# The second plain chunk prepares the fast weights in another order: loads first, high parts later

## The chip, the cores and the metric

The kernel runs on one core of a Trainium2 chip. The metric is the device time of one execution in microseconds (us), the median of the runs shown. TensorE (PE) multiplies matrices, VectorE (DVE) and ScalarE (ACT) work on elements, GpSimd (POOL) does little here, and SyncE (SP) issues every transfer. Each engine, SP's queue of transfers too, works in the order in which its instructions were written.

## The reference

The reference is sigmoid attention followed by a block of Fourier mixing, layer norm and a feed-forward network, for 8 sequences of 448 tokens and a width of 768:

```
x  = sigmoid(q k^T / 8 - log 448) v            (12 heads of 64, joined)
u  = x + real(fft(fft(x, tokens), width))
un = (u - mean) / sqrt(var + 1e-6)
out = u + max(un w1, 0) w2                      (768 -> 3072 -> 768)
```

The weights come as float64, and the result must be better than one float16 product gives. So each operand of the feed-forward network is split into a high part (rounded to float16) and a low part (the rest, float16 again), and three products are summed: high by high, high by low, low by high.

## The kernel before, in words

The 3584 tokens are worked in 7 chunks of 512. First come attention and mixing; in them the first two chunks are normed. Then two *plain* chunks (c = 0 and 1) go through the feed-forward network with the ordinary three products, in 24 iterations f of 128 hidden columns each. The last five chunks use a *fast* scheme in which a 2 by 2 block product is made from 7 products instead of 8; for that it needs sums and differences of the weights' quarters.

Those sums are made while the second plain chunk runs, by `combine` (L666), one call per step n, for 24 weight chunks j = 0 to 23 (j % 2 tells w1 from w2, j // 2 the pair of 128 columns):

- n = 0: the load. A tile `cb` (tag "wr", **three buffers**, 768 KB) is read from `t_dram` (L670).
- n = 1: the sums. Four DVE subtractions in place, L678.
- n = 2: the high part `ch`, an ACT copy to float16 with the scale, L682, into a tile of tag "wt".
- n = 3: the low part `cl`, DVE, L687, into the next tile of tag "wt". That tag has **three buffers**, used in turn by ch and cl.
- n = 4: six stores to `w_dram` on SP's queue: ch and two copies of plain high weights, then cl and two copies of plain low weights (L696 to L698 for w1, L700 to L702 for w2).

An iteration f of the second chunk (loop at L767) writes on the engines, in this order: the up-projection on PE (`up_proj`, 18 matmuls into a PSUM bank `psh`), its evacuation (`evac`: `hh` on ACT, L596, and `hl` on DVE, L597), the steps of `combine` that the table `made_at` names, the steps of the first fast chunk's norm (`fast_norm`, table `norm_at`), and the down-projection of the iteration before (`down_proj`, 18 matmuls that read hh and hl). The banks of `psh` are two, and the norm's transposes `pst` (L726, iterations 6 to 8 and 17 to 19) take a bank from the same two; ACT empties those into `U` (L727). The norm's casts to float16 are L739 (ACT) and L743 (DVE). `pin()` at the end of an iteration fixes the written order on each engine.

There are 24 weight chunks for 20 iterations, so four iterations take two of them. Chunk j has its turn in iteration f(j): 1, 2, 3, 4, 5, 5, 6, 7, 8, 8, 9, 10, 11, 11, 12, 13, 14, 14, 15 and so on to 20. The doubles are the chunks 4 and 5, 8 and 9, 12 and 13, 16 and 17. Before the change, chunk j is loaded in iteration f(j) − 1, summed and rounded (n = 1, 2) in f(j), and its low part and stores (n = 3, 4) come in f(j) + 1. Within an iteration all of this stands behind the evacuation: first the low parts and stores of the earlier chunk, then the load of the next, then sums and high part.

Of the kernel before, what the change touches and what calls it, by code (L numbers as in the profile page):

```python
# [44 lines left out]
NPLAIN = 2  # L45
# [13 lines left out]
def spectral_attention_ffn(tc, q, k, v, w1, w2, cd, cs, ident_in, out):  # L59
# [8 lines left out]
    with ExitStack() as top:  # L68
# [19 lines left out]
        if True:  # L88
# [356 lines left out]
            def prep_step(k, n):  # L445

                loads = []
                for d in range(1, 5):
                    if k + d < len(order) and (k + d, 0) not in prepped and not loadable(k + d, k):
                        break  # L450
                    loads.append((d, 0))
                for d, m in (loads, ((1, 1),), ((0, 2), (-1, 4)), ((0, 3),))[n]:
                    if k + d < len(order) and (k + d, m) not in prepped:
                        prepped.add((k + d, m))
                        prep_w(*order[k + d], m)
# [114 lines left out]
        with ExitStack() as fast, ExitStack() as st, ExitStack() as early:  # L570
# [12 lines left out]
            def up_proj(c, f, part=range(NCC)):  # L583
                uh, ul = uts[c]
                if (c, f) not in hs:
                    hs[c, f] = ps_h.tile([128, 512], F32, tag="m", name="psh")
                for m in part:
                    for n, (l, r) in enumerate(((w1h, uh), (w1h, ul), (w1l, uh))):
                        nc.tensor.matmul(  # L589
                            hs[c, f], l[f][:, m], r[:, m], start=(m == n == 0), stop=(m == NCC - 1 and n == 2))  # L590

            def evac(c, f):
                ps = hs[c, f]
                hh = up.tile([128, TW], F16, tag="hh", name="hh")
                hl = up.tile([128, TW], F16, tag="hl", name="hl")
                nc.scalar.activation(hh, ps, AF.Relu)  # L596
                nc.vector.scalar_tensor_tensor(  # L597
                    out=hl, in0=ps, scalar=0.0, in1=hh, op0=ALU.max, op1=ALU.subtract)
                hs[c, f] = (hh, hl)

            def down_proj(c, f):
                hh, hl = hs.pop((c, f))
                for n, cuts in enumerate(BANKS):
                    for i, lo, hi, at in cuts:
                        cols = slice(i * 128, (i + 1) * 128)

                        for m, (l, r) in enumerate(((hh, w2h), (hh, w2l), (hl, w2h))):
                            nc.tensor.matmul(  # L608
                                po[n][:, at:at + hi - lo], l[:, cols], r[f][:, lo:hi],
                                start=(f == 0 and m == 0 and at == 0),  # L610
                                stop=(f == NFC - 1 and m == 2 and at + hi - lo == 512))
                    if f == NFC - 1:
                        finish(c, n)
# [3 lines left out]
            def residual(c, g):  # L617
                u = wpre.tile([128, DM, 2], I32, tag="wr", name="ur", bufs=3).bitcast(F32)
                urs[c, g] = u = u.rearrange("p n w -> p (n w)").rearrange("p (i n) -> p i n", i=2)
                r0 = c * TW + g * 256  # L620
                nc.sync.dma_start(u, u_dram[r0:r0 + 256, :].rearrange("(i p) n -> p i n", p=128))
# [22 lines left out]
            while units or act_next or dve_next or sp_next:  # L644
# [4 lines left out]
                n = step % MIX_STEP  # L649
# [16 lines left out]
            def combine(i, p, n):  # L666

                if n == 0:
                    made[i, p] = t = wpre.tile([128, 4, 384], F32, tag="wr", name="cb", bufs=3)
                    nc.sync.dma_start(t.rearrange("p s n -> p (s n)"), t_dram[i, p].rearrange("p j n -> p (j n)"))  # L670
                elif n == 1:
                    t = made[i, p]
                    for o, x, y, op in (
                            ((1, 0, 1, ALU.add), (0, 2, 0, ALU.subtract),
                             (2, 1, 2, ALU.subtract), (3, 3, 2, ALU.subtract)),
                            ((2, 3, 2, ALU.subtract), (3, 1, 3, ALU.subtract),
                             (1, 1, 2, ALU.subtract), (0, 0, 1, ALU.subtract)))[i]:
                        nc.vector.tensor_tensor(out=t[:, o], in0=t[:, x], in1=t[:, y], op=op)  # L678
                elif n == 2:
                    t = made[i, p]  # L680
                    h = wpre.tile([128, 4, 384], F16, tag="wt", name="ch", bufs=3)
                    nc.scalar.activation(h, t, AF.Copy, scale=wsc[:, i:i + 1])  # L682
                    made[i, p] = t, h
                elif n == 3:
                    t, h = made[i, p]
                    l = wpre.tile([128, 4, 384], F16, tag="wt", name="cl", bufs=3)
                    nc.vector.scalar_tensor_tensor(  # L687
                        out=l, in0=t, scalar=wsc[:, i:i + 1], in1=h, op0=ALU.mult, op1=ALU.subtract)
                    made[i, p] = h, l
                else:  # L690
                    for j, (x, b) in enumerate(zip(made.pop((i, p)), ((w1h, w1l), (w2h, w2l))[i])):
                        to = w_dram[i, p][:, j]
                        b = [(b[f].rearrange("p c f -> p (c f)") if i == 0 else b[f]).rearrange(
                            "p (s n) -> p s n", s=2) for f in (2 * p + 1, 2 * p)]
                        if i == 0:
                            nc.sync.dma_start(to[:, 3:7], x)  # L696
                            nc.sync.dma_start(to[:, 0:1], b[0][:, 1:2])
                            nc.sync.dma_start(to[:, 1:3], b[1])  # L698
                        else:
                            nc.sync.dma_start(to[:, 0:4], x)  # L700
                            nc.sync.dma_start(to[:, 4:6], b[0])
                            nc.sync.dma_start(to[:, 6:7], b[1][:, 0:1])  # L702
# [44 lines left out]
            def load_w(i, P):  # L747
                if P < NP * (NCK - NPLAIN):
                    ws[i, P] = t = fw[i].tile([128, 2, 7, 384], F16, tag="ws", name="ws", bufs=(2, 4)[i])
                    nc.sync.dma_start(t, w_dram[i, P % NP])  # L750


            norm_at, made_at = {}, {}
            for j in range(NFC):
                f = 1 + j - (j > 4) - (j > 8) - (j > 12) - (j > 16)
                made_at.setdefault(f - 1, []).append((j, 0))
                made_at.setdefault(f, []).extend((j, n) for n in (1, 2))
                made_at.setdefault(f + 1, []).extend((j, n) for n in (3, 4))
            for x in made_at.values():
                x.sort(key=lambda x: (x[1] < 3, x[1] > 0, x))  # L760
            for tp in range(2):
                for f, steps in enumerate(((0,), (), (1, 2), (3, 4, 5, 6, 7), (8, 9), (), (10,), (11,), (12,),
                                           (13, 14), (15, 16), (17,))):
# [1 line left out]
            prev = None  # L765
            for c in range(NPLAIN):
                for f in range(NFC):  # L767
                    if (c, f) not in hs:
                        up_proj(c, f)
                    for n in range(2):  # L770
                        if c == 0 and slot <= len(order):
                            for step in range(4):
                                prep_step(slot, step)
                            slot += 1
                        if n == 0 and (c or f):
                            evac(c, f)
                    if f in (NFC - 3, NFC - 2):
                        residual(c, f - NFC + 3)
                    if c == NPLAIN - 1:
                        for j, n in made_at.get(f, ()):  # L780
                            combine(j % 2, j // 2, n)
                    if c == NPLAIN - 1:
                        for tp, n in norm_at.get(f, ()):
                            fast_norm(NPLAIN, tp, n, ps_h)
                    if prev is not None:
                        down_proj(*prev)
                    prev = (c, f)
                    pin()
                    if c == NPLAIN - 1 and f == NW1 + 1:
                        early.close()  # L790
                        fw.append(fast.enter_context(tc.tile_pool(name="fw1", bufs=1)))
                        h_pool = fast.enter_context(tc.tile_pool(name="h_pool", bufs=4))
                    if c == NPLAIN - 1 and f in (NFC - 4, NFC - 2):
                        load_w(0, (f - NFC + 4) // 2)
# [217 lines left out]
```

## Time and profile before

| what | value |
|---|---|
| median of 3 runs | 1744.54 us (1743.26 to 1745.85) |
| span of the profiled execution | 1744.9 us |
| PE busy | 1659.8 us, 95% of the span |
| DVE busy | 1296.0 us, 74% |
| ACT busy | 601.7 us, 34% |
| second plain chunk, 694 to 892 us | 198.0 us, PE busy 182.59 |
| 24 loads `cb`, 768 KB each | 6.4 us to landing (median) |
| 24 stores of `ch`, 384 KB each | 4.9 us to landing (median) |

The profile is one execution. In its views a row of a timeline gives the start in us, the duration, the engine, the line, the operation with out<-in, the count, and in brackets how long the engine had been idle before and what ended that. A row "SPq" is a transfer being issued; its landing is told by the view of the transfers. A releaser is inferred: where two things end together, the row names one of them.

### The profile page before, as it was taken

The numbers are of one execution on the slowest core, as the hardware profiler recorded it, in microseconds if no ns is written. First come the engines' busy times: TensorE is split into PE (matmuls) and PEld (weight loads), VectorE is DVE, ScalarE is ACT, GpSimd is POOL, SyncE is SP. The second block draws the span as 40 slices with busy tenths as digits, with TensorE's granted clock in tenths as the row PEclk, the third lists the DMA queues.
The fourth block names the chain that finished last, engine by engine and source line by source line (L and its number), as shares of the span: only waits on it lengthen the run. The fifth ranks groups of instructions, "written<-read, shape, count | busy, mean of one in ns | idle before, by whom it ended". The sixth has DMA issues, their size and how long they took to land. (4 is left out here: it accounts for less than half of the span.)

```text
span 1744.9 us, 27688 instructions
## 1 busy us (share of the span) xinstructions
PE 1659.8 (95%) x10996; PEld 1070.3 (61%) x10996; DVE 1296.0 (74%) x2481; ACT 601.7 (34%) x767; POOL 201.8 (12%) x220
## 2 busy tenths in 40 slices
PE   8999999997879999998899999999999999999997
PEld 4555555554544445554467777777777777777774
DVE  4556677866788884768557888788878888887768
ACT  5444444443334441232224332323232333223221
POOL 4534543443300000000000000000000000000000
PEclk9999999998999999999999999999999999999999
DMA  7666766874477663788876555655565665665561
GB/s 237 224 218 202 244 215 223 266 222 125 151 247 245 227 213 145 252 321 282 280 275 268 208 227 206 252 220 224 201 256 218 227 234 205 249 239 222 202 245 50
DMA packets 109140, 391.02 MB, mean 224 GB/s; under 512 B 23522, under 2 KB 49363, under 8 KB 93523
## 3 DMA queue, kind: packets, MB, share of 16 engines
q1 hardware_dynamic: 109010, 389.26, 63.4%
q8 instruction: 86, 1.41, 0.3%
q14 instruction: 44, 0.35, 0.1%
HBM read 312.15 MB, written 73.92 MB: 221 GB/s over the span
## 5 line engine op out<-in xcount | busy, mean ns | idle before, releaser
L870 PE MATMUL pso<-ws,H 128*128 128x384 f16 x2520 | 422.6, 326 | 0.9 <-DVE H L825 0.8
L819 PE MATMUL psf<-ut,ws 128*128 128x256 f16 x3780 | 422.1, 273 | 1.1 <-DVE ur L629 1.1
L819 PEld LDWEIGHTS <-ws 128*128 128x128 f16 x3780 | 369.8, 98 | 50.4 <-issue 1.4
L870 PEld LDWEIGHTS <-H 128*128 128x128 f16 x2520 | 246.4, 98 | 155.8 <-DVE H L825 1.1
L136 ACT ACTIVATE a<-sc 112x900 f32<-112x900 f32 x192 | 166.8, 918 | 154.2 <-PE sc L132 153.9
L879 DVE TENSOR_TENSOR acc<-pso,acc 128x384 f32<-128x384 f32 x350 | 181.6, 548 | 19.1 <-PE pso L870 19.1
L844 ACT ACTIVATE F<-F 128x1024 f32<-128x1024 f32 x60 | 63.5, 1058 | 332.1 <-DVE F L825 332.1
L152 PE MATMUL av<-a,vr 112*64 112x450 f32 x768 | 171.7, 569 | 3.5 <-DVE xT L161 3.5
L825 DVE TENSOR_TENSOR H<-F,H 128x1024 f16<-128x1024 f32 x120 | 129.4, 1087 | 47.0 <-ACT H L854 47.0
L589 PE MATMUL psh<-ut,w1h 128*128 128x512 f16 x504 | 152.1, 384 | 5.9 <-DVE hl L597 5.9
L608 PE MATMUL po<-w2h,hh 128*128 128x512 f16 (+1 forms) x384 | 128.9, 336 | 19.0 <-ACT hh L596 16.3
L825 DVE TENSOR_TENSOR F<-X,psf 128x256 f32<-128x256 f32 x240 | 97.8, 417 | 51.6 <-PE psf L819 48.9
L854 ACT ACTIVATE H<-F 128x1792 f16<-128x1792 f32 x60 | 101.8, 1697 | 88.6 <-DVE F L825 88.6
L608 PE MATMUL po<-w2h,hl 128*128 128x512 f16 (+1 forms) x384 | 128.5, 335 | 1.0
L608 PE MATMUL po<-w2l,hh 128*128 128x512 f16 (+1 forms) x384 | 128.5, 335 | 0.0
L608 PEld LDWEIGHTS <-hh 128*128 128x128 f16 x768 | 76.2, 100 | 71.5 <-ACT hh L596 21.0
L161 DVE TENSOR_SCALAR xT<-av 128x450 f32<-128x450 f32 x48 | 30.0, 625 | 115.5 <-PE av L152 115.5
L825 DVE TENSOR_TENSOR F<-F 128x256 f32<-128x256 f32 x240 | 91.1, 421 | 17.3 <-ACT F L844 12.9
L597 DVE SCALAR_TENSOR_TENSOR hl<-psh,hh 128x512 f16<-128x512 f32 x48 | 33.1, 690 | 94.7 <-ACT hh L596 94.5
L132 PE MATMUL sc<-qh,kh 64*112 64x450 f32 x384 | 82.6, 426 | 20.0 <-ACT a L136 15.3
L152 PEld LDWEIGHTS av<-a,vr 112*64 112x64 f32 x768 | 48.0, 140 | 84.1 <-issue 70.0
L589 PE MATMUL psh<-ut,w1l 128*128 128x512 f16 x252 | 96.5, 383 | 0.0
(105 smaller groups left out, 1977.2 us busy)
## 6 DMA issues: line engine op xcount, KB each, us to landing
ws<-w_dram SPq DMA_DIRECT2D x120, 1344.0 KB, 6.1
wr<-w_in SPq DMA_DIRECT2D x74, 768.0 KB, 6.0
cb<-t_dram SPq DMA_DIRECT2D x24, 768.0 KB, 6.4
t_dram<-wt SPq DMA_DIRECT2D x38, 384.0 KB, 2.6
qr<-q_in SPq DMA_DIRECT2D x48, 225.0 KB, 4.3
kr<-k_in SPq DMA_DIRECT2D x48, 224.0 KB, 3.6
vr<-v_in SPq DMA_DIRECT2D x24, 448.0 KB, 4.6
spare<-w_in SPq DMA_DIRECT2D x12, 768.0 KB, 4.7
```

The costliest lines, as they stand in the source:

```text
L132: nc.tensor.matmul(ps[:CP, j, :SQ], split[g, 1, kn][h, c * CP:(c + 1) * CP], split[g, 0, qn][h], start=(n == 0), stop=(n == 2))
L136: nc.scalar.activation(a, ps[:CP, :, :SQ], AF.Sigmoid, bias=-math.log(S), scale=1.0 / math.sqrt(D))
L152: nc.tensor.matmul(ps[j * D:(j + 1) * D, :SQ], vr[:, c, h * D:(h + 1) * D], a[:, j], start=(c == 0), stop=(c == 3))
L589: nc.tensor.matmul(hs[c, f], l[f][:, m], r[:, m], start=(m == n == 0), stop=(m == NCC - 1 and n == 2))
L597: nc.vector.scalar_tensor_tensor(out=hl, in0=ps, scalar=0.0, in1=hh, op0=ALU.max, op1=ALU.subtract)
L608: nc.tensor.matmul(po[n][:, at:at + hi - lo], l[:, cols], r[f][:, lo:hi], start=(f == 0 and m == 0 and at == 0), stop=(f == NFC - 1 and m ...
L819: nc.tensor.matmul(ps[:, :TH], w[:, x, a, m * 128:(m + 1) * 128], ut[y][:, b, m], start=(m == n == 0), stop=(m == n == 2))
L825: nc.vector.tensor_tensor(out=o, in0=x, in1=y, op=op)
L844: nc.scalar.activation(F[:, 0:4], F[:, 0:4], AF.Relu)
L854: nc.scalar.activation(hts[P][:, 0], F[:, 1:8], AF.Copy)
L870: nc.tensor.matmul(ps[:, :384], H[:, x, a, tp * 128:(tp + 1) * 128], w[:, y, b], start=(j == n == 0), stop=(j == 1 and n == 2))
L879: later(0, lambda: nc.vector.tensor_tensor(out=to, in0=ps[:, :384], in1=to, op=ALU.add))
```

## The change

Each step gets a place within the iteration: 0 is ahead of the up-projection, 1 and 2 are behind the evacuation, in that order. The load of chunk j goes to place 0 of iteration f(j) − 1 (it stood behind the stores there), the high part goes to place 0 of iteration f(j) + 1 (it stood behind the sums in f(j)), low part and stores stay in f(j) + 1, and the sums stay in f(j), behind them.

```
-                made_at.setdefault(f - 1, []).append((j, 0))
-                made_at.setdefault(f, []).extend((j, n) for n in (1, 2))
-                made_at.setdefault(f + 1, []).extend((j, n) for n in (3, 4))
-            for x in made_at.values():
-                x.sort(key=lambda x: (x[1] < 3, x[1] > 0, x))
+                made_at.setdefault((f - 1, 0), []).append((j, 0))
+                made_at.setdefault((f + 1, 0), []).append((j, 2))
+                made_at.setdefault((f + 1, 1), []).extend((j, n) for n in (3, 4))
+                made_at.setdefault((f, 2), []).append((j, 1))
...
                 for f in range(NFC):
+                    if c == NPLAIN - 1:
+                        for j, n in made_at.get((f, 0), ()):
+                            combine(j % 2, j // 2, n)
                     if (c, f) not in hs:
                         up_proj(c, f)
...
                     if c == NPLAIN - 1:
-                        for j, n in made_at.get(f, ()):
-                            combine(j % 2, j // 2, n)
+                        for k in (1, 2):
+                            for j, n in made_at.get((f, k), ()):
+                                combine(j % 2, j // 2, n)
```

The order of the instructions on PE and on DVE is the same before and after. On SP's queue and on ACT it differs. First SP's queue at the double of chunks 4 and 5, iteration 6, before; `ch_6411` and `cl_6466` are the high and low part of chunk 4, `ch_6417` and `cl_6474` those of chunk 5, and `cb_6482` is the load of chunk 7. The brackets list the engines and earlier transfers that a transfer waits for; a wait that an earlier one in the queue covers is not repeated.

```order
376 L696 DMA w_dram_62<-cl_6466 128x1536 [waits DMAHW7_49,DVE_49]
377 L697 DMA w_dram_62<-w1l5_4333 128x384 [waits DMAHW0_49]
378 L698 DMA w_dram_62<-w1l4_4332 128x768 [waits DMAHW1_49]
379 L700 DMA w_dram_62<-ch_6417 128x1536 [waits DMAHW2_49,Activation_49]
380 L701 DMA w_dram_62<-w2h5_4555 128x768 [waits DMAHW3_49]
381 L702 DMA w_dram_62<-w2h4_4554 128x384 [waits DMAHW4_49]
382 L700 DMA w_dram_62<-cl_6474 128x1536 [waits DMAHW5_49,DVE_49]
383 L701 DMA w_dram_62<-w2l5_4576 128x768 [waits DMAHW6_49]
384 L702 DMA w_dram_62<-w2l4_4575 128x384 [waits DMAHW7_49]
385 L670 DMA cb_6482<-t_dram_61 128x1536 [waits DMAHW0_49]
```

The store of the high part of chunk 4 stands three rows ahead of this piece and waits for ACT alone; the load of chunk 7 stands behind all stores of chunks 4 and 5. The same place after; here `cb_6443` is the load of chunk 7, `ch_6439` and `cl_6468` are the parts of chunk 4:

```order
372 L702 DMA w_dram_62<-w2l2_4350 128x384 [waits DMAHW3_49]
373 L670 DMA cb_6443<-t_dram_61 128x1536 [waits DMAHW4_49,DVE_49,Activation_49]
374 L696 DMA w_dram_62<-ch_6439 128x1536 [waits DMAHW5_49]
375 L697 DMA w_dram_62<-w1h5_4319 128x384 [waits DMAHW6_49]
376 L698 DMA w_dram_62<-w1h4_4318 128x768 [waits DMAHW7_49]
377 L696 DMA w_dram_62<-cl_6468 128x1536 [waits DMAHW0_49]
```

The load of chunk 7 has moved ahead of both stores of chunk 4, and the waits for ACT and DVE have moved from those stores to the load.

Second, ACT in iterations 5 to 8, before; `ch_6411` and `ch_6417` are the high parts of chunks 4 and 5, `ch_6488` and `ch_6559` those of 6 and 7, `hh_6462`, `hh_6539` and `hh_6610` belong to iterations 6, 7 and 8:

```order
380 L682 ACTIVATE ch_6411<-cb_6338,wsc_65 128x1536
381 L682 ACTIVATE ch_6417<-cb_6340,wsc_65 128x1536
382 L596 ACTIVATE hh_6462<-psh_6443 128x512
383 L682 ACTIVATE ch_6488<-cb_6405,wsc_65 128x1536
384 L727 ACTIVATE U_6061<-pst_6490 128x4x128
385 L596 ACTIVATE hh_6539<-psh_6520 128x512
386 L682 ACTIVATE ch_6559<-cb_6482,wsc_65 128x1536
387 L727 ACTIVATE U_6061<-pst_6561 128x4x128
388 L596 ACTIVATE hh_6610<-psh_6591 128x512
```

And after, where the high parts of chunks 4 to 7 are `ch_6439`, `ch_6441`, `ch_6518` and `ch_6589`:

```order
380 L682 ACTIVATE ch_6439<-cb_6307,wsc_65 128x1536
381 L682 ACTIVATE ch_6441<-cb_6309,wsc_65 128x1536
382 L596 ACTIVATE hh_6464<-psh_6445 128x512
383 L727 ACTIVATE U_6061<-pst_6488 128x4x128
384 L682 ACTIVATE ch_6518<-cb_6374,wsc_65 128x1536
385 L596 ACTIVATE hh_6543<-psh_6524 128x512
386 L727 ACTIVATE U_6061<-pst_6559 128x4x128
387 L682 ACTIVATE ch_6589<-cb_6443,wsc_65 128x1536
388 L596 ACTIVATE hh_6612<-psh_6593 128x512
```

Only ch and U have changed places; where an iteration has no work of the norm on ACT, the two orders are the same.

## The prediction

> **What bounds the kernel now.** I read the page's head first, then the table of windows, then the timelines of PE, ACT, DVE and the DMA queue where the second plain chunk combines the weights, and last the landing times of single transfers. Durations below come from the profiled execution; all that is shown of its time is its span, 0.4 us over the median of the runs, 1744.54 us, so the sum is made on the median.
>
> ```profile
> span 1744.9 us, 27688 instructions
> ```
>
> The edit touches the iterations between about 694 and 892 us. The table of windows, cut where TensorE stops (columns: length, then busy time and instructions of PE, PEld, DVE, ACT, POOL, then the granted clock, the DMA share and GB/s):
>
> ```profile
> 734.00:754.00 20.00, 15.83 (x78) 8.13 (x76) 11.04 (x14) 6.66 (x7) 0.00 (x0) 0.91 0.86 305
> 790.00:816.00 26.00, 21.36 (x97) 9.97 (x96) 19.25 (x30) 7.75 (x7) 0.00 (x0) 0.87 0.89 306
> 832.00:854.00 22.00, 15.40 (x71) 7.51 (x70) 11.70 (x15) 6.15 (x7) 0.00 (x0) 0.84 0.89 306
> 854.00:892.00 38.00, 38.00 (x208) 20.27 (x207) 20.28 (x32) 11.56 (x17) 0.00 (x0) 1.00 0.80 283
> ```
>
> In the last of these windows PE is busy all the time at full clock: there the stage is bound by TensorE and nothing that moves on ACT, DVE or the queue matters. In the first three PE idles 4.2, 4.6 and 6.6 us and the clock is below 1. Those three stops are what the change can give back; and each new stop is what it can cost. TensorE's timeline there:
>
> ```profile
> 744.85 1.12 PE L726 MATMUL pst<-ident,U 128*128 128x128 f32 x4 [3.87 <-ACT U L727]
> ...
> 747.68 0.35 PE L608 MATMUL po<-w2h,hh 128*128 128x256 f16 x1
> ...
> 750.68 0.59 PE L589 MATMUL psh<-ut,w1h 128*128 128x512 f16 x2
> ...
> 778.36 0.38 PE L608 MATMUL po<-w2h,hh 128*128 128x512 f16 x1
> ...
> 806.87 0.61 PE L608 MATMUL po<-w2h,hh 128*128 128x512 f16 x1 [3.97 <-ACT hh L596]
> ...
> 812.60 0.32 PE L608 MATMUL po<-w2h,hh 128*128 128x256 f16 x1
> ...
> 834.22 0.66 PE L726 MATMUL pst<-ident,U 128*128 128x128 f32 x4 [0.98 <-DVE hl L597]
> ...
> 844.39 1.01 PE L589 MATMUL psh<-ut,w1h 128*128 128x512 f16 x2 [5.62 <-DVE hl L597]
> ...
> 850.28 0.38 PE L589 MATMUL psh<-ut,w1l 128*128 128x512 f16 x1
> ```
>
> Call the stops A (744.85), B (806.87) and C (844.39). After each, matmuls run at about half speed until the second row shown for it: 2.9, 5.8 and 5.9 us, so 1.5, 2.9 and 2.9 us more are lost, 2.4 on average. After the idle 0.98 us there is none. By the Trainium skill, page "TensorE: Matmul & The Clock Gate", section "What's actually happening", the array drops to half clock after an idle window of some 3.4 us and needs such a time of work to come back; the trace agrees in kind, and with that figure a stop would cost 1.7 us more instead of 2.4 and a stop under 3.4 us nothing. The sum below would then be 0.7 less in double 1 and 1.2 less in double 2, +7.9.
>
> All three stops hang on one serial chain: DVE makes the sums of one weight chunk, ACT its high part, and behind it in ACT's order stands the activation that TensorE needs. ACT, then DVE:
>
> ```profile
> 742.74 1.57 ACT L682 ACTIVATE ch<-cb,wsc 128x1536 f16<-128x1536 f32 x1 [6.58 <-DVE cb L678]
> 744.22 0.58 ACT L727 ACTIVATE U<-pst 128x512 f32<-128x512 f32 x1
> 744.70 0.59 ACT L596 ACTIVATE hh<-psh 128x512 f16<-128x512 f32 x1
> ...
> 762.45 1.58 ACT L682 ACTIVATE ch<-cb,wsc 128x1536 f16<-128x1536 f32 x1 [0.72 <-DVE cb L678]
> 763.93 0.58 ACT L727 ACTIVATE U<-pst 128x512 f32<-128x512 f32 x1
> 764.41 0.59 ACT L596 ACTIVATE hh<-psh 128x512 f16<-128x512 f32 x1
> ```
>
> ```profile
> 736.80 3.66 DVE L687 SCALAR_TENSOR_TENSOR cl<-cb,wsc,ch 128x1536 f16<-128x1536 f32 x2
> ...
> 745.31 0.69 DVE L597 SCALAR_TENSOR_TENSOR hl<-psh,hh 128x512 f16<-128x512 f32 x1 [2.61 <-ACT hh L596]
> ...
> 756.07 1.81 DVE L687 SCALAR_TENSOR_TENSOR cl<-cb,wsc,ch 128x1536 f16<-128x1536 f32 x1
> ...
> 773.67 0.69 DVE L597 SCALAR_TENSOR_TENSOR hl<-psh,hh 128x512 f16<-128x512 f32 x1
> ...
> 795.23 1.81 DVE L687 SCALAR_TENSOR_TENSOR cl<-cb,wsc,ch 128x1536 f16<-128x1536 f32 x1
> 800.65 1.82 DVE L687 SCALAR_TENSOR_TENSOR cl<-cb,wsc,ch 128x1536 f16<-128x1536 f32 x1 [3.61 <-DMA w_dram<-ch]
> ...
> 825.43 3.66 DVE L687 SCALAR_TENSOR_TENSOR cl<-cb,wsc,ch 128x1536 f16<-128x1536 f32 x2
> ...
> 833.47 0.69 DVE L597 SCALAR_TENSOR_TENSOR hl<-psh,hh 128x512 f16<-128x512 f32 x1 [0.95 <-ACT hh L596]
> ...
> 839.14 2.34 DVE L678 TENSOR_TENSOR cb<-cb 128x384 f32<-128x384 f32 x4 [3.25 <-DMA cb<-t_dram]
> 843.65 0.69 DVE L597 SCALAR_TENSOR_TENSOR hl<-psh,hh 128x512 f16<-128x512 f32 x1 [2.17 <-ACT hh L596]
> ```
>
> **What the change moves.** No instruction is added or removed; PE's and DVE's orders stay as they are. Two things move.
>
> On ACT only the high parts and the copies of the norm (U, and the casts of ut) change places, in iterations 6, 7, 8, 10, 17 to 19. Elsewhere "half an iteration later" is the same place in ACT's order. Stop A goes: the copy of U that PE waited for stood behind ch, which stood 6.58 us waiting for its sums, and now stands ahead.
>
> On the DMA queue each load moves ahead of the stores of the chunk two before it. In the four places where two chunks share an iteration (chunks 4 and 5, 8 and 9, 12 and 13, 16 and 17), the load of chunk j+3 needs the buffer of chunk j, which the low part (cl) of j reads last. So the queue now stands at that load until the first low is done, and only then issues the store of the first high part, which was issued long before. The second low writes into the buffer that this store reads (three buffers for the high and low parts): DVE must wait until it has landed. In the old order the two lows run as one block (the "x2" rows at 736.80 and 825.43); once, at 800.65, DVE already waits 3.61 us for exactly this store. What a store takes right behind a load: the queue's rows with two stores issued 0.7 us behind a load (and the store of high 12, at 795.37), the landing times of the first and the second of these two, and the spread of all 24:
>
> ```profile
> 743.66 0.49 SPq L670 DMA_DIRECT2D cb<-t_dram  x1
> 744.34 0.32 SPq L696 DMA_DIRECT2D w_dram<-ch  x1
> ...
> 772.49 0.51 SPq L670 DMA_DIRECT2D cb<-t_dram  x1
> 773.18 0.32 SPq L696 DMA_DIRECT2D w_dram<-ch  x1
> ...
> 795.37 0.38 SPq L696 DMA_DIRECT2D w_dram<-ch  x1
> ```
>
> ```profile
> w_dram<-ch SPq DMA_DIRECT2D x1, 384.0 KB, 5.6
> ```
>
> ```profile
> w_dram<-ch SPq DMA_DIRECT2D x1, 384.0 KB, 5.9
> ```
>
> ```profile
> DMA to landing us min/median/max: 2.9/4.9/8.5
> ```
>
> Between the median of all (4.9, most of them not behind a load) and 5.9 I take 5.4: in the new order less is in flight ahead of the pair than at 744.34. So from the end of the first low to the start of the second pass 0.7 + 5.4 = 6.1 us. By the Trainium skill, page "DMA: Bandwidth & Descriptors", section "Anatomy of one DMA — SWDGE (gpsimd) path", a transfer takes some 2.0 us and its bytes at 436 GB/s, 2.9 us for 384 KB; the least store agrees (2.9 us), the two behind a load do not. With 2.9 the hold is 3.6 us, and the sum is that of the first rival.
>
> **The sum, double by double,** against where PE stands in the old trace.
>
> 1. Chunks 4 and 5. The first low ends at 736.80 + 1.81 = 738.6, the second starts at 744.7 instead of 738.6. Behind it stand, as before, sums, high part, hh, hl; without the copy of U (744.70 − 744.22 = 0.5) hl would have come at 744.8, so now at 750.9, ending 751.6. PE's up-projection 8 waits for its bank: 751.6 instead of 750.68, +0.9. PE, no longer held at A, will have idled longer than the 3.87 us there, so half clock follows: +2.4. Together **+3.3**.
> 2. Chunks 8 and 9. The store of high 7 is held too, by the low at 756.07: 757.9 + 6.1 = 764.0, and high 9, which reuses a buffer, starts there instead of at 762.45; the copy of U no longer stands behind it, so hh moves from 764.41 to 765.5: 1.1. Then the second low: 6.1. hl goes from 773.67 to 780.9, ending 781.6; PE wanted it two matmuls (0.4) after 778.36: 2.8 us of stop. Whether 2.8 us halves the clock lies between 0.98 (no) and 3.87 (yes): half of 2.4. **+4.0**.
> 3. Chunks 12 and 13. The first low ends at 797.0, the second starts at 803.1 instead of 800.65: stop B grows by 2.5. **+2.5**.
> 4. Chunks 16 and 17. The second low starts 6.1 later, so hl moves from 833.47 to 839.6 and PE's transposes from 834.22 to 840.3: a stop of 7.1 us with half clock behind it. But the load of chunk 19 now goes out at 827.3 instead of behind the stores, and the 3.25 us at 839.14 go: those sums follow hl (0.69) and low (1.81) at 842.1, and hl 17 comes 4.5 us after them as before (843.65 − 839.14): 846.6, ending 847.3. Up-projection 18 starts 2.9 later than 844.39, but without stop C's half clock (2.9); the slow matmuls ahead of it end by then. **0.0**.
>
> 3.3 + 4.0 + 2.5 + 0.0 = **+9.8 us**: 1754.3 us. From iteration 18 on PE is the bound (the last window), so nothing more is added or given back. The earlier loads of the single chunks save DVE waits which PE doesn't see; costed at nothing, and where that cover is thin (the 3.25 us) it is in step 4. With stores landing in 4.9 and 1.5 us of clock per stop I get about +5; with 5.9 and 2.9 about +15, and 2 more if the second highs 5 and 13 are held like 9: 1749 to 1762.
>
> **Rivals.**
>
> *The held stores land fast.* With the queue empty behind the load, 2.9 us as the fastest store: a hold of 3.6. Double 1: PE starts at 749.1, −1.6, and 2.4 for the clock; double 2: hl 3.1 later is inside PE's 4 us of slack; 3: the second low at 800.6, as before; 4: hl 17 ends at 844.8, up-projection 18 starts 0.4 late and without C's clock loss, −2.5. Sum 0.8 − 2.5 = −1.7: 1742.8, no measurable change. The page "DMA: Bandwidth & Descriptors" of the Trainium skill would have it so. It decides below about 3.5 us of landing. The one such store that DVE already waits for speaks against it: issued at 795.37, it let the low start at 800.65. Chance 0.15.
>
> *The load does not hold the queue.* If the wait for the buffer is over when the queue gets there, the stores go out as before and the gains stand alone: A with its clock 5.4, 3.25 of C and perhaps its clock: about −9, 1735.5, faster. Against it: in the new order the store of the low behind the load has no wait for DVE of its own any more, so the load's wait covers that low. Chance 0.07.
>
> *Stores land as late as the worst.* 8.5 us, 3.1 more per hold and two holds in double 2: +15.5, 1770. The 8.5 stood behind two loads at once; the new order brings pairs of loads only in other iterations. Chance 0.06.
>
> **The numbers.** A measurement tells about 0.2%, 3.5 us, from no change. Forecast 0.72, nearly all of it slower by more than that (0.69; 0.03 at its low end within it). First rival: 0.12 within, 0.03 faster. Faster 0.10, same 0.15, slower 0.75. The range from 1743 to 1762 leaves out the second and third rival and a part of the first's lower half, together 0.2.
>
> **What would show it.** In the changed profile: four waits of DVE cl for the DMA w_dram<-ch, of 5 to 7 us each, in place of one of 3.61; the waits of DVE cb for loads gone; PE stops at an up-projection near 752, a down-projection near 785 and 817, the transposes near 850, and none at A's transposes; ACT's U right behind hh. Wrong if the cl waits are under 4 us (first rival) or missing (second), or if PE stops in iterations without a double.

## The result, and the profile after

The changed kernel takes 1761.69 us (median of 4 runs, 1759.00 to 1761.86) and the kernel before 1745.10 us beside it: a ratio of 1.0090, 95% interval 1.0076 to 1.0105. It is slower, by 16.6 us where 9.8 were predicted; the median lies inside the range by 0.3 us.

The page of the changed kernel's profile opens with its span (12.1 us more than before), and its table of windows shows PE bound again from iteration 18 on:

```profile
span 1757.0 us, 27670 instructions
```

```profile
866.00:904.00 38.00, 38.00 (x208) 20.25 (x207) 21.59 (x33) 11.08 (x16) 0.00 (x0) 1.00 0.78 282
```

A clean length of the stage is the time from hl of iteration 2 to hl of iteration 23 (starts of these DVE rows): 701.89 to 891.77 = 189.9 us before, 699.52 to 903.83 = 204.3 after. So the stage loses 14.4 us. The profiled execution reached it 2.37 us earlier than before's, which is why the spans differ by less.

DVE after, the second lows of the four doubles (first the first low of double 1 for comparison), then the lows of the iterations just ahead of the doubles:

```profile
735.77 1.81 DVE L687 SCALAR_TENSOR_TENSOR cl<-cb,wsc,ch 128x1536 f16<-128x1536 f32 x1
743.98 1.82 DVE L687 SCALAR_TENSOR_TENSOR cl<-cb,wsc,ch 128x1536 f16<-128x1536 f32 x1 [6.41 <-DMA w_dram<-ch]
...
778.20 1.82 DVE L687 SCALAR_TENSOR_TENSOR cl<-cb,wsc,ch 128x1536 f16<-128x1536 f32 x1 [6.18 <-issue]
...
811.92 1.82 DVE L687 SCALAR_TENSOR_TENSOR cl<-cb,wsc,ch 128x1536 f16<-128x1536 f32 x1 [5.66 <-DMA w_dram<-ch]
...
845.57 1.82 DVE L687 SCALAR_TENSOR_TENSOR cl<-cb,wsc,ch 128x1536 f16<-128x1536 f32 x1 [5.60 <-DMA w_dram<-ch]
```

```profile
725.11 1.82 DVE L687 SCALAR_TENSOR_TENSOR cl<-cb,wsc,ch 128x1536 f16<-128x1536 f32 x1 [1.55 <-DMA w_dram<-w1l]
...
759.49 1.82 DVE L687 SCALAR_TENSOR_TENSOR cl<-cb,wsc,ch 128x1536 f16<-128x1536 f32 x1 [1.19 <-DMA w_dram<-ch]
...
793.54 1.82 DVE L687 SCALAR_TENSOR_TENSOR cl<-cb,wsc,ch 128x1536 f16<-128x1536 f32 x1 [1.62 <-DMA w_dram<-ch]
...
827.47 1.82 DVE L687 SCALAR_TENSOR_TENSOR cl<-cb,wsc,ch 128x1536 f16<-128x1536 f32 x1 [1.83 <-DMA w_dram<-ch]
```

Four holds of 5.6 to 6.4 us stand where before had one of 3.61. The smaller holds of 1.2 to 1.8 are new as well. The DMA queue shows what makes the large one: the load of chunk 7 goes out when the first low ends (735.77 + 1.81 = 737.58), the store of high 4 behind it. That store's landing time, and the one's of double 2, follow:

```profile
737.64 0.32 SPq L670 DMA_DIRECT2D cb<-t_dram  x1
738.00 0.43 SPq L696 DMA_DIRECT2D w_dram<-ch  x1
...
747.21 5.76 SPq L670 DMA_DIRECT2D cb<-t_dram  x2
753.01 0.43 SPq L696 DMA_DIRECT2D w_dram<-ch  x1
```

```profile
w_dram<-ch SPq DMA_DIRECT2D x1, 384.0 KB, 5.8
```

```profile
w_dram<-ch SPq DMA_DIRECT2D x1, 384.0 KB, 5.7
```

738.00 + 5.8 = 743.8, and the second low starts at 743.98. At double 2, where the low's row names no transfer, 772.44 + 5.7 = 778.1, and the low starts at 778.20. The Trainium skill, page "DMA: Bandwidth & Descriptors", section "Anatomy of one DMA — SWDGE (gpsimd) path", says that a transfer's semaphore wait is served by the issuing sequencer before it hands the transfer on; the queue rows agree. The same section of the Trainium skill gives figures for GpSimd's path that make an estimate of 2.9 us for 384 KB; on SP's queue behind a load the trace has 5.8 and 5.7. For the stores of doubles 3 and 4 it has no landing time.

ACT after, the second highs of the doubles, and hh and U at the end of double 1:

```profile
733.07 1.57 ACT L682 ACTIVATE ch<-cb,wsc 128x1536 f16<-128x1536 f32 x1 [2.28 <-DMA w_dram<-ch]
...
749.56 0.58 ACT L596 ACTIVATE hh<-psh 128x512 f16<-128x512 f32 x1
750.04 0.59 ACT L727 ACTIVATE U<-pst 128x512 f32<-128x512 f32 x1
...
767.51 1.57 ACT L682 ACTIVATE ch<-cb,wsc 128x1536 f16<-128x1536 f32 x1 [2.34 <-DMA w_dram<-ch]
...
801.75 1.57 ACT L682 ACTIVATE ch<-cb,wsc 128x1536 f16<-128x1536 f32 x1 [2.54 <-DVE ut L743]
...
835.46 1.57 ACT L682 ACTIVATE ch<-cb,wsc 128x1536 f16<-128x1536 f32 x1 [2.32 <-DVE mv L345]
```

All four second highs stand still for 2.3 to 2.5 us, not only the one of chunk 9. And PE, every stop over 1 us in the stage:

```profile
735.66 0.59 PE L589 MATMUL psh<-ut,w1h 128*128 128x512 f16 x2 [1.40 <-ACT U L727]
...
750.68 1.01 PE L589 MATMUL psh<-ut,w1h 128*128 128x512 f16 x2 [6.63 <-ACT U L727]
...
784.41 0.39 PE L608 MATMUL po<-w2h,hh 128*128 128x512 f16 x1 [3.74 <-ACT hh L596]
...
803.87 0.39 PE L608 MATMUL po<-w2h,hh 128*128 128x512 f16 x1 [1.74 <-ACT hh L596]
...
818.13 0.61 PE L608 MATMUL po<-w2h,hh 128*128 128x512 f16 x1 [6.01 <-ACT hh L596]
...
837.58 0.39 PE L608 MATMUL po<-w2h,hh 128*128 128x512 f16 x1 [1.15 <-ACT hh L596]
...
852.51 1.12 PE L726 MATMUL pst<-ident,U 128*128 128x128 f32 x4 [6.68 <-DVE hl L597]
```

Together 27.4 us of idle, against 14.4 in before (3.87 + 3.97 + 0.98 + 5.62). The large stops lie at the four places named in the prediction; each small one is in the iteration of a double, ahead of a large one. Windows of 6.0 us from the restarts after the four stops over 3 us show the granted clock:

```profile
784.40:790.40 6.00, 5.87 (x25) 2.87 (x26) 5.90 (x9) 4.10 (x8) 0.00 (x0) 0.72 0.58 156
750.68:756.68 6.00, 6.00 (x18) 2.34 (x18) 4.05 (x6) 1.57 (x1) 0.00 (x0) 0.63 0.53 147
818.13:824.13 6.00, 6.00 (x22) 2.94 (x23) 5.86 (x10) 1.27 (x1) 0.00 (x0) 0.57 0.65 198
852.51:858.51 6.00, 6.00 (x24) 3.45 (x25) 3.81 (x5) 2.00 (x3) 0.00 (x0) 0.59 1.01 364
```

Losses of (1 − clock) × 6.0, in the order of the rows: 1.7, 2.2, 2.6 and 2.5 us, where the prediction took 2.4 for a long stop and half of that for the one near 785.

### The profile page after: what moved, and what is told of

Read it like the earlier page. It is cut to its first block, busy times and chain, and to the rows that moved or that the text cites. A ratio compares the mean times of both kernels' runs of the same rounds, so it can differ in the third digit from the quotient of the medians.

```text
span 1757.0 us, 27670 instructions
## 1 busy us (share of the span) xinstructions
PE 1662.0 (95%) x10996; PEld 1070.8 (61%) x10996; DVE 1296.3 (74%) x2481; ACT 601.9 (34%) x767; POOL 201.8 (11%) x220
```

## The experiments

Theory 1 is the prediction's: a load that stands ahead of the stores holds the queue until its buffer is free, the held store of a high part keeps its buffer, and the next part waits for that. Theory 2: the later high part costs, since ACT's work moves towards PE's. Theory 3: the earlier loads take transfer time from others. Edits are shown against the changed kernel. "Stage" is hl 2 to hl 23 of the profiled execution, as above. Each ratio is to the kernel before as it ran on the same chip in the same session (medians 1745.10, 1746.05, 1747.45 and 1745.64 us); the sessions ran on different chips, so kernels of different sessions are compared by their ratios.

| kernel | median us | ratio to before (95%) | stage us |
|---|---|---|---|
| before | | | 189.9 |
| changed | 1761.69 | 1.0090 (1.0076–1.0105) | 204.3 |
| changed_again | 1764.41 | 1.0114 (1.0094–1.0133) | 204.7 |
| high_only | 1741.69 | 0.9978 (0.9963–0.9993) | 183.6 |
| load_only | 1771.26 | 1.0159 (1.0142–1.0175) | 218.0 |
| spare_after | 1752.21 | 1.0037 (1.0022–1.0052) | 196.1 |
| load_mid | 1739.90 | 0.9969 (0.9956–0.9983) | 184.1 |
| four_early | 1752.41 | 1.0031 (1.0021–1.0041) | 198.0 |
| four_back | 1746.45 | 0.9996 (0.9985–1.0007) | 188.6 |
| four_early_spare | 1744.27 | 0.9995 (0.9985–1.0006) | 186.4 |
| high_behind_hh | 1733.96 | 0.9924 (0.9908–0.9940) | 179.6 |
| high_behind_hh_spare | 1734.95 | 0.9932 (0.9917–0.9947) | 177.3 |

**high_only: the high part later, the loads as before.**

```
-                made_at.setdefault((f - 1, 0), []).append((j, 0))
+                made_at.setdefault((f - 1, 2), []).append((j, 0))
```

> The loads are back behind the stores (the queue's order of the kernel before); only the high part stands half an iteration later. Theory 1 (the load that waits for its buffer holds the stores behind it on the queue, and the second low part waits for the held store): no hold, stop A gone, 1736 to 1741 us. Theory 2 (the later high part itself is what costs: it stands behind the norm's copies on ACT, so low part and stores come later): as the changed kernel, 1755 to 1762. Theory 3 (the earlier loads take the transfer engines from the stores): as theory 1.

Faster than before by 0.22%, stage 6.3 us shorter. DVE runs the two lows of double 1 as one block again:

```profile
735.52 3.66 DVE L687 SCALAR_TENSOR_TENSOR cl<-cb,wsc,ch 128x1536 f16<-128x1536 f32 x2
```

The later high part is a gain, a little smaller than expected (1741.69, where 1736 to 1741 was); theory 2 falls. All of the loss comes with the loads.

**load_only: the loads earlier, the high part with its sums as before.**

```
-                made_at.setdefault((f + 1, 0), []).append((j, 2))
...
-                made_at.setdefault((f, 2), []).append((j, 1))
+                made_at.setdefault((f, 2), []).extend((j, n) for n in (1, 2))
```

> Only the loads are moved ahead of the stores; the high part stays behind its sums. Theory 1: the four holds of about 6 us, and stop A made longer because the copy of U still stands behind the held chain: slower than the changed kernel, 1761 to 1769 us. Theory 2: as the kernel before, 1745. Theory 3: as the changed kernel, 1757 to 1762.

The slowest of all, and 2 us above what was expected. The holds are there; the old place of the high part makes them dearer. ACT and PE behind double 1:

```profile
752.90 1.57 ACT L682 ACTIVATE ch<-cb,wsc 128x1536 f16<-128x1536 f32 x1 [13.09 <-DVE cb L678]
754.38 0.58 ACT L727 ACTIVATE U<-pst 128x512 f32<-128x512 f32 x1
```

```profile
755.01 1.12 PE L726 MATMUL pst<-ident,U 128*128 128x128 f32 x4 [10.38 <-ACT U L727]
```

The held low delays the sums, the high part stands waiting for them ahead of U, and stop A grows from 3.87 to 10.38 us. The later high part, which puts U first, takes a part of this away (6.63 us of stop are left at double 1 in the changed kernel). The two halves of the change interact: the later high part shields TensorE from what the earlier loads hold up. Their ratios multiplied, 0.9978 × 1.0159, would give 1.0137; together they give 1.0090.

**spare_after: a buffer of their own for the first highs of the doubles.**

```
+                    first = i == 0 and p in (2, 4, 6, 8)
-                    h = wpre.tile([128, 4, 384], F16, tag="wt", name="ch", bufs=3)
+                    h = (wpre.tile([128, 4, 384], F16, tag="w1p", name="ch") if first
+                         else wpre.tile([128, 4, 384], F16, tag="wt", name="ch", bufs=3))
```

> The changed kernel, order of all engines kept, but the first high part of each double (chunks 4, 8, 12, 16) gets a buffer of its own, so the second low part no longer writes where the held store reads. Theory 1: the queue is held as before, but DVE's four waits of 5.6 to 6.4 us go; the small waits in front of the doubles stay; 1744 to 1752 us. Theories 2 and 3: nothing they name has changed, 1757 to 1762.

The buffer is one under the tag of `w1p`, whose weights are done with by then. The second low no longer needs the held store, and the load still goes out when the first low ends (at 739.36). Stage 8.2 us shorter than the changed kernel's, though the median ends just above what was expected. DVE, then ACT, at double 1:

```profile
737.49 3.54 DVE L689 SCALAR_TENSOR_TENSOR cl<-cb,wsc,ch 128x1536 f16<-128x1536 f32 x2
740.94 2.33 DVE L678 TENSOR_TENSOR cb<-cb 128x384 f32<-128x384 f32 x4
```

```profile
747.48 1.57 ACT L684 ACTIVATE ch<-cb,wsc 128x1536 f16<-128x1536 f32 x1 [10.15 <-issue]
```

The lows are one block, so the 6.4 us were the buffer. But the sums are done at 743.3 and the next high starts 4.2 us later. It takes, in turn, a buffer that another store behind the load reads. The row names no transfer here, so this is inferred: from the three buffers' turn, and from a store of the same iteration (the first low's, issued at 741.30) that landed at 747.33, 0.15 us ahead of this high. The hold has partly moved on. Early loads as such are not the cost: theory 3 does not explain why the block comes back.

**load_mid: each load behind the high part's stores, ahead of the low part's.**

```
                     for j, (x, b) in enumerate(...):
+                        if n == 5 - j:
+                            continue
...
-                made_at.setdefault((f - 1, 0), []).append((j, 0))
-                made_at.setdefault((f + 1, 1), []).extend((j, n) for n in (3, 4))
+                made_at.setdefault((f + 1, 1), []).extend((j, n) for n in (3, 4, 5))
+            for j in range(NFC):
+                f = 1 + j - (j > 4) - (j > 8) - (j > 12) - (j > 16)
+                x = made_at.setdefault((f - 1, 1), [])
+                x.insert((2 if x and x[0][1] == 3 else 0) + ((j - 1, 0) in x), (j, 0))
```

> The changed kernel, but each load stands behind the first high part's three stores and ahead of the low part's. Loads go out about as early as in the changed kernel (they wait for the same low part), the held store no longer stands behind them. Theory 1: no wait for a held store over 4 us, 1737 to 1744 us. Theory 2: high parts as late as in the changed kernel, 1757 to 1762. Theory 3: the loads as early, 1755 to 1762.

Of the first chunk's six stores only the low part's three are left behind the load, and the loss is gone. The load of chunk 7 goes out 2.7 us after hl of its iteration started (2.5 in the changed kernel), so it is still early. DVE's lows at doubles 1 and 3 (where before has its wait of 3.61; the 4.30 is over the 4 us that were expected at most):

```profile
736.10 3.67 DVE L687 SCALAR_TENSOR_TENSOR cl<-cb,wsc,ch 128x1536 f16<-128x1536 f32 x2 [0.19 <-DMA w_dram<-cl]
...
797.42 1.82 DVE L687 SCALAR_TENSOR_TENSOR cl<-cb,wsc,ch 128x1536 f16<-128x1536 f32 x1 [4.30 <-DMA w_dram<-ch]
```

What hurts is that the high part's store stands behind the load, not that the load is early. With spare_after this is theory 1, by two edits that take away different ends of it.

**four_early and four_back: which loads.** First only loads 7, 11, 15 and 19 (those whose buffer the first low of a double reads) ahead, then only those four behind.

```
-                made_at.setdefault((f - 1, 0), []).append((j, 0))
+                made_at.setdefault((f - 1, 0 if j in (7, 11, 15, 19) else 2), []).append((j, 0))
```

```
+                made_at.setdefault((f - 1, 2 if j in (7, 11, 15, 19) else 0), []).append((j, 0))
```

> The changed kernel, but only the loads of chunks 7, 11, 15 and 19 (those that hold the first high part's store of a double) stay ahead of the stores; all others go back behind them. If the four holds that the prediction priced are the whole cost: as the changed kernel, 1758 to 1762 us. If a part of it comes from the loads in the other iterations, which hold the stores of the high parts 3, 7, 11 and 15 and through them the second high part of the double: 4 to 7 us less, 1752 to 1757.

> The other way round: only those four loads go behind the stores, all others stay ahead. If the four holds are the whole cost: as with all loads back, 1737 to 1742 us. If the other iterations cost 4 to 7 us: 1743 to 1748.

Both medians lie where the second expectation of each run has them: a part of the cost is not the four's. In stage lengths over high_only's 183.6, one profiled execution each: the four loads cost 14.4 us, the other twenty 5.0, all together 20.7. The four are most of it, the others a quarter, and they nearly add up (19.4). In the medians the parts add up less well: 0.53% and 0.18%, against 1.12% for all, so the shares are rough. DVE in four_early shows the four large holds by themselves:

```profile
740.71 1.82 DVE L687 SCALAR_TENSOR_TENSOR cl<-cb,wsc,ch 128x1536 f16<-128x1536 f32 x1 [6.45 <-DMA w_dram<-ch]
...
772.48 1.82 DVE L687 SCALAR_TENSOR_TENSOR cl<-cb,wsc,ch 128x1536 f16<-128x1536 f32 x1 [6.27 <-DMA w_dram<-ch]
...
803.68 1.82 DVE L687 SCALAR_TENSOR_TENSOR cl<-cb,wsc,ch 128x1536 f16<-128x1536 f32 x1 [6.38 <-DMA w_dram<-ch]
...
838.01 1.82 DVE L687 SCALAR_TENSOR_TENSOR cl<-cb,wsc,ch 128x1536 f16<-128x1536 f32 x1 [8.42 <-DMA w_dram<-ch]
```

**four_early_spare: four_early with the buffer of spare_after.**

```
-                made_at.setdefault((f - 1, 0), []).append((j, 0))
+                made_at.setdefault((f - 1, 0 if j in (7, 11, 15, 19) else 2), []).append((j, 0))
...
+                    first = i == 0 and p in (2, 4, 6, 8)
```

> The run with only the loads of chunks 7, 11, 15 and 19 ahead of the stores, and a buffer of its own for the first high part of each double. If those four loads cost only through the second low part that waits for the held store: all of their cost goes, as with all loads back, 1738 to 1744 us. If they cost in another way too (the queue standing still, the second high part's store coming late, traffic): 1746 to 1753.

The median, 1744.27, lies at the edge of the first expectation. 11.6 of the four loads' 14.4 us of stage go (198.0 to 186.4), and in the medians about two thirds (0.31% slower to 0.05% faster, where high_only is 0.22% faster). No wait of a low for a store is left. Of the rest, one piece is seen: ACT's high 6, DVE's sums being done at 740.32 + 2.33 = 742.65:

```profile
746.75 1.57 ACT L684 ACTIVATE ch<-cb,wsc 128x1536 f16<-128x1536 f32 x1 [10.04 <-DMA w_dram<-cl]
```

```profile
749.35 0.59 PE L589 MATMUL psh<-ut,w1h 128*128 128x512 f16 x2 [3.98 <-ACT U L729]
```

It waits 4.1 us more, now for a store by the row's own name (a low's; by the turn of the buffers it would be the one of high 5, issued behind the same load), and U behind it lets PE stop for 3.98 instead of 6.35 us (four_early, at 747.40).

**high_behind_hh: loads as before, the high part behind the evacuation's hh.** In the changed kernel ch stands ahead of hh in the iteration, so a late store or late sums hold hh as well.

```
-                made_at.setdefault((f - 1, 0), []).append((j, 0))
-                made_at.setdefault((f + 1, 0), []).append((j, 2))
+                made_at.setdefault((f - 1, 2), []).append((j, 0))
+                made_at.setdefault((f + 1, 1), []).append((j, 2))
```

> Loads behind the stores, and the high part later still: behind the evacuation of the next iteration instead of ahead of it, so that hh never stands behind a high part that waits for its sums. If the chain sums, high part, hh is what stops TensorE: stops A, B and C all go or shrink below 1 us, 1727 to 1735 us. If what bounds there is DVE or the transfers, the stops move to another wait and the time stays at that of the high part alone, 1740 to 1744.

0.9924: faster than both kernels, and the time that was expected. ACT's and PE's waits in the stage (total, times, longest):

```profile
ACT hh L596 <- PE psh L589: 90.2, 20, 7.2
```

```profile
PE po L608 <- DVE hl L597: 4.5, 2, 2.5
PE psh L589 <- DVE hl L597: 3.5, 1, 3.5
```

hh waits for nothing but PE itself, and PE idles 8.0 us in three stops (2.01, 2.46 and 3.45) instead of 27.4 in seven; not one is for ACT. That all stops go or shrink below 1 us did not come true.

**high_behind_hh_spare: the same with the buffer of spare_after.**

```
-                made_at.setdefault((f + 1, 0), []).append((j, 2))
+                made_at.setdefault((f + 1, 1), []).append((j, 2))
...
+                    first = i == 0 and p in (2, 4, 6, 8)
```

> As the run before, with a buffer of its own for the first high part of each double, so that the second low part waits for no store of the same iteration. If the remaining stops come from that wait: 1724 to 1732 us, 2 to 4 less than the run before; if not, the same as it.

The expected gain is not in the medians: 0.9932 against 0.9924 (the stage of the profiled execution is 2.3 us shorter). PE's stops stay at 2.20, 2.50 and 4.29 us, all for hl. In DVE's order hl stands there behind sums and the norm's small steps; the sums of the first and the third stop waited 4.14 and 3.81 us for their load. No run tried to take this away.

**changed_again: the changed kernel once more, with no edit.**

> The changed kernel once more, with more runs, beside the kernel before on the same chip: how large the loss is. The first measurement gave a ratio of 1.009 (1.0076 to 1.0105), the profiled executions 14.4 us more in the second plain chunk, ratio 1.0083. Between 1.0075 and 1.0105, 1758 to 1763 us.

A little more than expected: 18.8 us slower in the medians, with a stage of 204.7 us (14.8 over before's). So some 14.5 us are shown to be lost in the stage; the medians say 2 to 4 us more. From hl 23 to the end all twelve profiled executions take 853.1 to 853.5 us, so it does not lie there. hl 2 starts between 697.8 and 704.1 us in them, and the profiled execution of the changed kernel is its fastest one (1759.00 us): the 2 to 4 us are within what the stretch ahead of the stage varies by, and that the change costs them is not shown.

## Why the prediction was right, and where it was short

**The path: right.** The load holds the queue, the store of the first high goes out after the first low, the second low waits for it. Predicted hold 0.7 + 5.4 = 6.1 us; measured 6.41, 6.18, 5.66, 5.60, mean 6.0. Taking the row of a store behind a load (5.6 to 5.9), not the fastest of 2.9, decided the sign, and with it against the rival of fast stores. load_mid and spare_after show the path by removing it. The second rival falls with the same rows: the queue does stand. One reading behind the 5.4 was thinner than it said: the 2.9, 4.9 and 8.5 are called the spread of all 24 stores, but the trace of the kernel before has a landing time for nine of them.

**Stop A: right.** There is no stop at those transposes, and high_only shows that the later high part gains. That it also shields from the held sums (load_only) was not in the prediction. The stop of double 1 ends, by its row, with the copy of U (750.04 + 0.59), where the prediction had the end of hl; the two are 0.2 us apart.

**Double by double.** The mark is the start of the first up-projection behind a double's stop and its half clock, in the timeline of PE before and after. The delay is the difference plus the 2.37 us, and a double's part is how much it grows:

| double | mark before, after | delay | part | predicted | what differs |
|---|---|---|---|---|---|
| 1 | 758.91, 761.05 | 4.5 | +4.5 | +3.3 | 1.40 us stop at 735.66 |
| 2 | 782.26, 790.29 | 10.4 | +5.9 | +4.0 | stop of 3.74, not 2.8; clock 1.7, not 1.2; 0.5 not placed |
| 3 | 813.62, 824.59 | 13.3 | +2.9 | +2.5 | 1.74 us stop at 803.87 |
| 4 | 855.48, 867.54 | 14.4 | +1.1 | 0.0 | 1.15 us stop at 837.58 |

The parts make 14.4 us, where the sum had 9.8. PE's idle time and clock give nearly the same: 12.9 us more idle (27.4 − 14.4, rounded) and 1.7 more for the clock (9.0 against 7.3, the three stops of the prediction). So the sum was 4.6 us short of what the stage lost, and the median fell inside the range by little; by changed_again (18.8 us) it would lie 1.3 us above it. The mechanism is shown, the hit of the range is partly luck.

**The mis-sized term.** The prediction priced the holds in the doubles' own iterations at chunk 9 alone (1.1 us) and left "2 more if the second highs 5 and 13 are held like 9" out of the sum. They were held, all four: 2.28, 2.34, 2.54 and 2.32 us on ACT, and behind them hh and U, with PE stops of 1.40, 1.74 and 1.15 us. In four_early, where the loads ahead of these stores are back, none of these three stops is there. The loads behind this are those outside the four (four_back puts 5.0 us of stage on them): "costed at nothing" holds for what they spare DVE, not for the stores that they stand in front of. The pair of loads at 747.21, for one, holds the queue for 5.76 us before the next store. The row names for highs 13 and 17 are DVE's. For these two the store is inferred: each of the four highs starts 5.7 to 6.0 us after the store of high 3, 7, 11 or 15 was issued (at 727.36, 761.74, 795.79 and 829.71).

**The clock.** 2.4 us for a long stop was about right (2.2, 2.6, 2.5 in the windows). Half of it for the stop of double 2 was too little: 1.7. That a stop's length decides, as the prediction's choice between 0.98 and 3.87 us has it, the runs do not bear out (see the last section). By the Trainium skill, page "TensorE: Matmul & The Clock Gate", section "What's actually happening", the array is back at full clock after some 3.4 us of work, which makes an estimate of 1.7 us per stop: one of the four agrees (1.7), the other three cost 2.2 to 2.6. The same section of the Trainium skill has half clock after an idle window of some 3.4 us; high_behind_hh has it after stops of 2.01 and 2.46 us.

**Not explained.** The 2 to 4 us by which the medians exceed the stage's loss, as above.

## What to carry to other kernels

A transfer that must wait for its buffer holds everything behind it on its queue, so moving a load ahead of stores has the price of those stores' readers and buffers; check which buffer each held store keeps, and who writes it next. Count this for every transfer moved, not only for the places with the longest hold: here the four worst loads made about 70% of the cost in the stage, and the twenty that looked harmless about a quarter. Work whose inputs can come late belongs behind what TensorE waits for on the same engine: with the high part there and the loads as before, the kernel was 0.8% faster than before.

## What the runs showed of the hardware

Half clock does not always begin at the restart. PE in the changed kernel after the stop of 3.74 us (row 784.41 above), matmuls of 256 columns:

```profile
785.36 0.27 PE L608 MATMUL po<-w2h,hh 128*128 128x256 f16 x1
...
786.00 0.42 PE L608 MATMUL po<-w2h,hl 128*128 128x256 f16 x1
...
789.32 0.27 PE L608 MATMUL po<-w2h,hh 128*128 128x256 f16 x1
```

It runs at full speed for some 1.4 us, then at half speed for 3.4. So the first row after a stop does not tell whether the clock was lost.

Nor does the stop's length tell it. Two stretches of high_behind_hh, with the stop of 2.01 us (798.63 to 800.64) inside the first, and two of four_back, whose border lies in the stop of 3.07 us (789.26 to 792.33); the granted clock is the third number from the end:

```profile
797.41:800.82 3.41, 1.40 (x7) 0.49 (x6) 3.07 (x6) 0.76 (x1) 0.00 (x0) 1.00 1.10 375
800.82:804.23 3.41, 3.41 (x12) 1.67 (x11) 1.82 (x1) 1.30 (x2) 0.00 (x0) 0.50 0.91 346
```

```profile
787.52:790.94 3.42, 1.74 (x9) 0.59 (x6) 2.82 (x6) 1.07 (x2) 0.00 (x0) 1.00 0.99 378
790.94:794.35 3.41, 1.90 (x11) 1.01 (x12) 2.04 (x2) 1.33 (x2) 0.00 (x0) 1.00 1.02 328
```

The shorter stop was followed by half clock, the longer one was not. Between 694 and 892 us of all twelve traces, half clock comes in stretches of 3.41 us or a multiple of it, in each trace on one grid (in the changed kernel from 748.25, 785.80, 816.52 and 850.65, which are 11, 9 and 10 times 3.41 us apart). Cut the traces on that grid: every stretch at full clock in which PE idled 2.0 us or more is followed by half clock, none with 1.90 us or less is, and of two in between (1.93 and 1.97 us) one is. So what counted in these runs is how much of a stop falls into one stretch of the grid. And the part of a half-clock stretch that lies inside the stop itself costs nothing: of the 6.83 us from 748.25, 4.40 come after the restart at 750.68, and the loss is 2.2.
